# Loading a projection's weights in four later pieces and adding products of constants, in a recurrent-memory and linear-attention kernel

## The chip, the cores and the metric

The kernel runs as one program on one core of a Trainium2 chip. The metric is device time in microseconds of one execution. A core has five engines with their own instruction streams: TensorE (PE in the profile, with its weight loads listed as PEld), VectorE (DVE), ScalarE (ACT), GpSimd (POOL) and SyncE (SP). Here SP only issues DMA transfers; ACT and POOL issue some too. All DMA engines of the core are shared by all of these queues.

## The reference, cut to what matters

The input x is 2048 rows of 512. Four blocks follow each other, A, B, A, B, and each adds its result to x after a layer norm.

```
# A: 64 segments of 32 rows, 8 memory rows carried from one segment to the next
for s in range(64):
    h = concat([mem, xs])                       # 8 + 32 rows
    q, k, v = h @ Wq, h @ Wk, h @ Wv            # 32 heads of 128
    o = softmax(mask(q @ k.T * scale)) @ v
    o = o @ Wo                                  # back to 512
    mem = o[:8]; outs.append(o[8:])
# B: linear attention, 32 heads of 16
q, k, v = split(x @ wqkv);  pq, pk = phi(q), phi(k)   # phi: t+1 if t>0 else exp(t)
kv = pk.T @ v;  z = sum(pk)
out = ((pq @ kv) / (pq @ z)) @ wo
```

The memory rows make A a chain: a segment can't begin before the one ahead of it has passed through the output projection. B needs all rows of a block before its own output can be formed, since kv and z are sums over all 2048 rows.

## The kernel before, in words

The weights Wq, Wk, Wv and Wo (4 MB each) stay in SBUF for the whole run. SP issues their loads first: Wk, Wq and Wv as one transfer each, then Wo in 16 transfers of 256 KB, then wqkv (1.5 MB), the projection of block B, as one transfer (`load`, lines 1950 to 1962). ACT issues the memory rows and the first 128 rows of x, POOL the next two tiles of x.

A step is one segment of A. It projects the 40 rows to keys and queries (`project`, products at L2154, further ones with the weights that stay loaded at L2042), copies the results out of PSUM (L1919 on ACT, L1920 on DVE) and turns them by DVE transposes (L2173). Values are projected in the same way. `mem_attention` handles the part on which the next segment's memory depends (L2278, L2270, then L2304, L2306 and L2318). `out_block` is the output projection, 64 products with Wo (L2408); its two halves are added (L2419) and `next_mem` (L2436) turns the 8 new memory rows into columns for the next step. `x_attention` does the other rows beside the next step.

Every fourth row of x (the last 8 of each segment) is projected for four segments at once, the "left" blocks. In the opening, three of these are done before or beside step 0 (`first_left_blocks`: keys "sk", queries "sq", values "leftv").

Block B runs four steps behind A: `b_in` takes a tile of 128 rows through its layer norm, projects it with wqkv (`rows_of`, L2582) and adds to the sums kva and za. Its first use of wqkv is at 109.3 us. When all rows are there, `b_mid` forms four matrices zf (L2714) for the denominators and km (L2699), multiplies km with wo into MB (four products, copied out by L1920 or L1919), and `b_out` makes each tile: denominators (a product with zf), logarithm and exponential on ACT (L2811, L2813), the quotient on DVE (L2814), four products with MB and the sum on DVE (L2818). In the last block all 16 tiles come after the last segment; this is "the last memory tile's chain" with what follows it.

What sets the order: every operation is a node with a due time and, for copies, an engine, both from a table written into the kernel (`PLACE`). `schedule` sorts the nodes by due time, gives PSUM banks in that order, and each engine executes its nodes in that order, waiting on semaphores where a node needs another engine's result. A due time is no wait: an engine goes on as soon as its data are there. So the table decides order, the engine of a copy, and the PSUM bank, and nothing else.

The functions that the change touches follow.

Of the kernel before, what the change touches and what calls it, by code (L numbers as in the profile page):

```python
# [16 lines left out]
    (0, -9, 'setup'): '2751 2752 1621 15060 15061 16711 17238 20254 20902 21335 26596 31128 31613 36233 37053 37678 40093 41399 42472 43512 44808 60645 14865 0 560 1120 2190 2750 3310 17835 18402 18743 18744 18748 18959 18960 19391 20038 20470 21117 21333 21981 22197 22628 24910 25947 26595 27242 27673 27674 27675 27892 27891 29832 31127 32422 35143 39577a 17834 18745v 0 32839 35503 35506 36229 36234 29400 18746 0 0 0 0 0 0 0 0 0 0 0 0 0 0 0 0 0 0 0 0 0 0 0 0 0 0 0 0 0 0 0 0 0 0 0 0 0 0 0 0 0 0 0 0 0 0 0 0 0 0 0 0 0 0 0 0 0 0 0 0 0 0 0 0 0 0 0 0 0 0 0 0 0 0 0 0 0 0 0 0 0 0 0 0 0 27889 27890',  # L17
    (0, -4, 'start'): '19607a',
    (0, -2, 'leftv'): '37698 39210 39672 40371 41400a 41831 42471 42962a 44807 44810',
    (0, -2, 'prep'): '14142 14864 15059 15391 15647 16712 18006v 18749a 19393a 20471v 17833v',  # L20
    (0, -2, 'prepl'): '13340 14063 16713 18747 22198 22843 25550a',
    (0, 0, 'kq0'): '19821 20469 20901 22411 29615 29831 31126 31611 22843a 35502 32197v 34321',
    (0, 0, 'kq1'): '20685 22627 23714 26377 27672 28320 30046 30262 28751a 36228 34684v 32840a 35139',
    (0, 0, 'lq'): '730981 734917 735345 736139 737902 739038 739581 745577',
    (0, 0, 'lx'): '725135',
    (0, 0, 'mem0'): '36230 36232 37051 37314 37677 39560 40092 44809 43119 44811',
    (0, 0, 'mem1'): '36231 36726 37679 37681 42962 43400 43719 44806 45734 46451',
    (0, 0, 'next'): '48918 48972 49238v',
    (0, 0, 'out'): '45447 45515 46452 46605 46882 47101 47370 47588 48015a 48443',
    (0, 0, 'ql'): '35504a 34436a',  # L30
    (0, 0, 'sk'): '19390 21116 22196 23282 23707v 24430',
    (0, 0, 'sq'): '29183 29399 30910 31773 32197a 32838',
    (0, 0, 'v'): '39211 40967 41398 41830 42470a 44812a',
    (0, 0, 'x'): '38130 38346 38692 39560 39576 41401 40094 42262 48015 43282 43341 46451 48409 50344a 57004v 45446 46824 47807 48297 51423a 50345v',
    (0, 0, 'xl'): '1620',
    (0, 1, 'kq0'): '49480 49911 50343 50775 51855v 52419 51639a 52056',
    (0, 1, 'kq1'): '52419 52419 52501 52717 51206 51422 51638 51854 53141a 53782 52934a 52717a 52992',
    (0, 1, 'lq'): '756403 760618 760834 761049 762164 763460 764413 769975',
    (0, 1, 'mem0'): '52933 53423 53994 53795 54262 55249 55828 55830 55827 56230',
    (0, 1, 'mem1'): '53994 54876 55248 55829 55831 56230 56623 57442 56840 57443',  # L40
    (0, 1, 'next'): '59643 59697 59962a',
    (0, 1, 'out'): '56622 57003 57221 57440 58377 58378 58379 58717 58970a 59168',
    (0, 1, 'ql'): '40264a 39209v',
    (0, 1, 'res'): '65669 65917',
    (0, 1, 'sk'): '18958 20037 21332 21980 24908a 25549',
    (0, 1, 'sq'): '26161 26593 27456 28967 33316a 33958',
    (0, 1, 'v'): '52991 53523 54263 54444 55085v 56275a',
    (0, 1, 'x'): '55899 56274 57221 57444 57581 58716 58036 58376 59643 58718 58719 58969 59850 62803v 70329a 58851 58910 59168 59961 60644a 61939a',
    (0, 2, 'kq0'): '60212 60643 61075 61507 63018v 63151 62587a 63020',
    (0, 2, 'kq1'): '62802 63017 63290 63507 61938 62154 62370 62586 64587a 64588 63019a 63289a 63717',  # L50
    (0, 2, 'leftv'): '40535 42262 43511 44806 45446a 46088 47102 47371a 53348 57441',
    (0, 2, 'lq'): '762163 762379 763027 763243 764661 765609 767779 770110',
    (0, 2, 'lx'): '730981',
    (0, 2, 'mem0'): '63449 64586 65177 64958 65549 65916 66408 66717 66931 67239',
    (0, 2, 'mem1'): '64958 65176 65548 65668 65918 66158 66930 67238 67867 67868',
    (0, 2, 'next'): '70328 70382 70962v',
    (0, 2, 'out'): '67869 67870 67907 68125 68344 68562 68780 68999 69606a 69853',
    (0, 2, 'prep'): '15988 16710 16904 17237 17493 17968 18401v 26594v 20255a 24909v 29184a',
    (0, 2, 'ql'): '54469v 58910v',
    (0, 2, 'res'): '73922 79787',  # L60
    (0, 2, 'sk'): '19174 20253 21548 23498 27457a 27893',
    (0, 2, 'sq'): '28104 30478 30694 32421 35141a 35865',
    (0, 2, 'v'): '63723 64155 64959 65670 65916a 66933v',
    (0, 2, 'x'): '66408 66932 67451 67866 68781 69470 69130 68999 70496 69605 69853 69853 70753 75955a 81212v 69853 70436 70495 70641 70961a 71496v',
    (0, 3, 'kq0'): '71496 71537 72185 72616 73265a 73923 73921a 74831',
    (0, 3, 'kq1'): '73048 73696 74552 74559 70963 71969 73911 74127 75207a 75956 74551a 74830a 75955',
    (0, 3, 'lq'): '735345 757243 757954 760402 761049 762743 765002 785076',
    (0, 3, 'mem0'): '75206 75265 75836 75637 76342 77046 77047 77387 77180 77582',
    (0, 3, 'mem1'): '76343 76344 76658 77180 77045 77386 77975 78306 78192 78668',
    (0, 3, 'next'): '81044 81098 81364v',  # L70
    (0, 3, 'out'): '77974 78355 78573 78988 79060 79784 79785 79786 80399a 80569',
    (0, 3, 'ql'): '70193v 73911a',
    (0, 3, 'res'): '81365 89404',
    (0, 3, 'sk'): '18742 19606 21764 23066 27894a 28105',
    (0, 3, 'sq'): '31612 34437 35140 35142 37052v 37314',
    (0, 3, 'v'): '73264 74775 75837 75957 76659v 77388a',
    (0, 3, 'x'): '77386 77673 78027 78573 78987 79783 79442 79923 81098 80569 81211 81270 81364 85987a 86151a 80398 81152 81441 81499 86277v 86751v',
    (0, 4, 'kq0'): '81611 82043 82474 83122 83986v 84485 84485a 85065',
    (0, 4, 'kq1'): '82906 84486 84850 84851 83554 83769 83985 84485 85497a 85914 84904a 84849a 85332',
    (0, 4, 'lq'): '767175 767779 768593 774744 778783 779388 780112 785508',  # L80
    (0, 4, 'lx'): '754821',
    (0, 4, 'mem0'): '85496 85986 86358 87108 87110 87762 88094 88805 88311 88806',
    (0, 4, 'mem1'): '86518 86576 87327 87109 88311 88474 89023 89841 89022 90059',
    (0, 4, 'next'): '92261 92315 92581v',
    (0, 4, 'out'): '89403 89621 89840 90058 90276 90495 90713 90931 91358a 91786',
    (0, 4, 'ql'): '83987a 84848v',
    (0, 4, 'res'): '95415 97436 87107 87326 87544 87874 88092 88585 88804 89185 90495a 90713 92827 92824 95198 94120 92826 96826 94983 95199 97493',
    (0, 4, 'sk'): '25730 27241 27888 28536 30695v 30911',
    (0, 4, 'sq'): '32205 36835 37051 37680 38693v 38846',
    (0, 4, 'v'): '85064 85914 86151 86751 87763v 88093a',  # L90
    (0, 4, 'x'): '88585 91150 92825 92828 92829 94984 94119 94550 95414 96708 96825 97316 98357 99061a 100805v 96766 97375 97865 98804 102000a 104112a',
    (0, 4, 'xl'): '3810',
    (0, 5, 'kq0'): '92823 93254 93686 94118 95416a 96886 94982a 96885',
    (0, 5, 'kq1'): '94549 94765 94981 95197 95413 95628 95844 96060 96277a 97435 97434a 96484a 97866',
    (0, 5, 'lq'): '762595 763890 764412 765003 768386 771109 775937 776686',
    (0, 5, 'mem0'): '97433 97492 98359 97864 98708 100009 100144 100187 100143 100549',
    (0, 5, 'mem1'): '98277 98277 98911 98358 100008 101159 101478 101787 102002 102149',
    (0, 5, 'next'): '104710 104764 105030v',
    (0, 5, 'out'): '101014 101478 101489 102406 102543 102761 102979 103256 103683a 104111',
    (0, 5, 'ql'): '96827v 97437a',  # L100
    (0, 5, 'res'): '112945 107325',
    (0, 5, 'sk'): '25946 26809 27025 28751 30970a 31611',
    (0, 5, 'sq'): '32197 35505 37682 38130 39599a 40371',
# [1690 lines left out]
def _build_kernel(nc, A_x, A_mem0, A_Wq, A_Wk, A_Wv, A_Wo, A_seg_len, B_wqkv, B_wo, out):  # L1794
# [119 lines left out]
    add = P.add  # L1914
# [132 lines left out]
    def tiled(pe, o, w, x, start, stop, loaded=False):  # L2047

        for j in range(4):
# [3 lines left out]
            else:  # L2053
                r = pe.matmul(o[q], w[:, q], x, start=start, stop=stop, skip_group_check=True, tile_position=(0, 32 * j))  # L2054
        return r

    SPIN = {}
    LATE = {0: (8, 9, 10, 11, 12, 13, 6, 7, 4, 5), 1: (4, 5, 6, 7)}
    def spin(layer, step, name, units, cols=512, fresh=0):

# [818 lines left out]
```

## Time and profile before

| what | us |
|---|---|
| median of three runs (1575.15 to 1579.79) | 1576.27 |
| the profiled execution's own time | 1580.13 |
| its span, from first to last instruction | 1578.4 |
| PE busy (share of the span) | 1511.5 (96%) |
| DVE busy | 1223.1 (77%) |
| ACT busy | 987.4 (63%) |
| PE share of the chain that ended last | 83% |

The profile is of one execution. Times in its views are counted from the first instruction. "Idle before" names what ended the idle time of an engine; "issue" there means that the engine waited for nothing that the profile shows. PEclk is the share of the TensorE clock that was granted. The queue named q8 is that of instruction fetches.

### The profile page before, as it was taken

The page shows a single profiled execution, that of the slowest core. Times are in us where ns is not written, and L with a number is a line of the kernel's source. Part 1 is how long each engine was busy: PE and PEld are TensorE (multiplying, and loading weights), DVE is VectorE, ACT ScalarE, POOL GpSimd, SP SyncE. Part 2 cuts the span into 40 slices and gives each one's busy share as a digit, 9 for nine tenths or more (in the row PEclk, how much of TensorE's full clock was granted, in tenths as well). Part 3 has the DMA queues.
Part 4 walks back from the last instruction along what each step waited for, and adds up shares of the span by engine and source line. Part 5 has one row for each costly group of instructions (what it writes and reads, how often), then busy time and mean ns, then how long its engine had stood idle before and what let it go on. Part 6 is the DMA issues. An engine that isn't in the chain of part 4 may idle for free.

```text
span 1578.4 us, 97381 instructions
## 1 busy us (share of the span) xinstructions
PE 1511.5 (96%) x48481; PEld 822.8 (52%) x40705; DVE 1223.1 (77%) x3536; ACT 987.4 (63%) x3043; POOL 197.2 (12%) x396
## 2 busy tenths in 40 slices
PE   5899999999999999999999999999999999999997
PEld 2445555555555555555545555555555455555554
DVE  4577878887777788777878787888877787777778
ACT  2566665656666666665666666666576666576665
POOL 2011110111111011111111110111101011110110
PEclk9999999999999999999999999999999999999999
DMA  9301010110000000101310111111101111001124
GB/s 381 104 20 20 17 33 20 27 24 23 21 18 16 22 24 24 24 17 30 62 32 17 26 25 20 25 29 21 31 10 27 27 27 23 23 20 20 34 42 134
DMA packets 84819, 60.69 MB, mean 38 GB/s; under 512 B 64121, under 2 KB 78777, under 8 KB 82873
## 3 DMA queue, kind: packets, MB, share of 16 engines
q1 hardware_dynamic: 71096, 37.58, 9.7%
q0 software_dynamic: 13152, 16.75, 3.9%
q8 instruction: 349, 5.72, 1.5%
q14 instruction: 62, 0.50, 0.1%
q10 hardware_dynamic: 160, 0.14, 0.0%
HBM read 25.57 MB, written 11.67 MB: 24 GB/s over the span
## 4 chain that ended last, share of the span: by engine, by line
PE 83%; DVE 8%; ACT 4%; DMA 3%; issue 1%; POOL 0%; SPq 0%; DVEq 0%
PE pb L2154 31%; PE pb L2042 21%; PE pb L2408 18%; PE pb L2054 8%; PE pb L2582 2%; ACT arena_sb L1919 2%; DMA Wq_sb<-in_A_Wq_dram 2%; PE pb L2270 1%; DMA dx_sb<-y_sb 1%; DVE arena_sb L1920 1%; PE pb L2347 1%; PE pb L2436 1%; DVE arena_sb L2173 1%; DVE y_sb L2419 1%; DVE st_sb L2092 1%
## 5 line engine op out<-in xcount | busy, mean ns | idle before, releaser
L1919 ACT ACTIVATE arena_sb<-pb 128x512 bf16<-128x512 f32 (+5 forms) x1180 | 530.8, 483 | 320.4 <-PE pb L2042 162.1
L1920 DVE CAST arena_sb<-pb 128x512 bf16<-128x512 f32 (+4 forms) x591 | 297.7, 512 | 93.7 <-PE pb L2042 51.1
L2154 PE MATMUL pb<-Wk_sb,arena_sb 128*32 128x512 bf16 x4192 | 364.4, 383 | 5.5 <-ACT arena_sb L1919 3.3
L2408 PE MATMUL pb<-Wo_sb,arena_sb 128*32 128x256 bf16 x10368 | 337.6, 273 | 4.4 <-DVE arena_sb L2318 2.1
L2173 DVE STREAM_TRANSPOSE arena_sb<-arena_sb 128x256 f32<-128x256 f32 x640 | 266.2, 432 | 48.7 <-ACT arena_sb L1919 41.2
L2054 PE MATMUL pb<-arena_sb 128*32 128x128 bf16 (+2 forms) x10800 | 277.0, 208 | 14.8 <-DVE arena_sb L1920 4.9
L2408 PEld LDWEIGHTS pb<-Wo_sb,arena_sb 128*32 128x32 bf16 x10368 | 258.1, 96 | 48.7 <-DVE arena_sb L2318 14.7
L1936 POOL DMA_DIRECT2D dx_sb<-y_sb x246 | 125.3, 513 | 1152.4 <-DVE y_sb L2419 627.0
L2054 PEld LDWEIGHTS pb<-arena_sb 128*32 128x32 bf16 x10800 | 190.1, 95 | 147.5 <-issue 33.3
L2154 PE MATMUL pb<-Wq_sb,arena_sb 128*32 128x512 bf16 x3088 | 259.5, 382 | 1.5 <-DMA Wq_sb<-in_A_Wq_dram 0.4
L2042 PE MATMUL pb<-Wv_sb,arena_sb 128*32 128x512 bf16 x2560 | 251.6, 378 | 0.1
L2154 PE MATMUL pb<-Wv_sb,arena_sb 128*32 128x512 bf16 x2560 | 251.5, 378 | 0.1
L2154 PEld LDWEIGHTS pb<-Wk_sb,arena_sb 128*32 128x32 bf16 x4192 | 112.9, 97 | 193.2 <-issue 102.6
L2042 PE MATMUL pb<-Wq_sb,arena_sb 128*32 128x512 bf16 x2032 | 199.3, 380 | 0.0
L2154 PEld LDWEIGHTS pb<-Wq_sb,arena_sb 128*32 128x32 bf16 x3088 | 83.8, 97 | 97.2 <-issue 44.4
L1919 ACT ACTIVATE outW_sb<-pb 64x256 f32<-64x256 f32 x142 | 53.6, 378 | 106.0 <-PE pb L2408 90.1
L2419 DVE TENSOR_TENSOR y_sb<-pb,outW_sb 64x256 bf16<-64x256 f32 x162 | 68.7, 424 | 50.1 <-ACT outW_sb L1919 45.4
L2358 DVE TENSOR_TENSOR arena_sb<-arena_sb,bo_sb 128x512 bf16<-128x512 bf16 x256 | 103.5, 416 | 2.4
L2318 DVE TENSOR_TENSOR arena_sb<-pb,arena_sb 128x128 bf16<-128x128 f32 x252 | 72.9, 290 | 36.3 <-ACT arena_sb L2306 12.2
L2154 PEld LDWEIGHTS pb<-Wv_sb,arena_sb 128*32 128x32 bf16 x2560 | 70.5, 95 | 53.6 <-issue 29.5
L2042 PE MATMUL pb<-Wk_sb,arena_sb 128*32 128x512 bf16 x928 | 92.5, 379 | 0.0
L2293 DVE TENSOR_TENSOR arena_sb<-arena_sb 128x256 bf16<-128x256 bf16 x252 | 70.2, 281 | 24.2 <-ACT arena_sb L2285 21.1
(122 smaller groups left out, 1804.9 us busy)
## 6 DMA issues: line engine op xcount, KB each, us to landing
Wk_sb<-in_A_Wk_dram SPq DMA_DIRECT2D x1, 4096.0 KB, 13.7
Wq_sb<-in_A_Wq_dram SPq DMA_DIRECT2D x1, 4096.0 KB, 24.4
Wv_sb<-in_A_Wv_dram SPq DMA_DIRECT2D x1, 4096.0 KB, 34.1
Wo_sb<-in_A_Wo_dram SPq DMA_DIRECT2D x16, 256.0 KB, 7.4
xs_scratch<-x_sb POOLq DMA_DIRECT2D x32, 128.0 KB, 2.7
pq_scratch<-arena_sb POOLq DMA_DIRECT2D x27, 128.0 KB, 2.5
x_sb<-xs_scratch POOLq DMA_DIRECT2D x16, 128.0 KB, 3.3
dx_sb<-y_sb SPq DMA_DIRECT2D x126, 12.0 KB
```

The lines of the kernel that those rows point to most:

```text
L1919: return e.activation(o() if callable(o) else o, i() if callable(i) else i, ACTF.Copy)
L1920: return e.tensor_copy(o() if callable(o) else o, i() if callable(i) else i)
L1936: add(eng, lambda e: e.dma_start(o, i), 0.55 if eng == "pool" else 0.66, reads=reads, writes=writes, dsem="%s%d" % (kind, k), lat=lat + (0 ...
L2042: return pe.add_instruction(mybir.InstMatmult(name=nc.get_next_instruction_name(), engine=mybir.EngineType.PE, ins=[pe.lower_ap(x), pe.low ...
L2054: r = pe.matmul(o[q], w[:, q], x, start=start, stop=stop, skip_group_check=True, tile_position=(0, 32 * j))
L2154: r = pe.matmul(o, blk[:, c, :], w, start=(c == 0), stop=(c == 3), tile_position=(0, 32 * j))
L2173: add("dve", lambda v: v.transpose(dst, src(img[:, k, :].bitcast(F32))), 0.445, reads=[("img", k, h) for h in range(2)], writes=[dkey])
L2293: add("dve", lambda v: v.tensor_tensor(Pm[:, k, :].rearrange("p (a j x) -> p a j x", a=2, j=4), PQ[:, r2, b, 0:64].rearrange("p (a x) -> p ...
L2318: add("dve", lambda v: v.tensor_tensor(oTb[:, s % NO, 16 * b:16 * b + 16, 0:8].rearrange("p (i j) q -> p j i q", i=4), heads(pv.f32()[:, 0 ...
L2358: add("dve", lambda v, b=b: v.tensor_tensor(Pbx[:, :, b, :].rearrange("p j (k x) -> p j k x", k=4), px[:, b, :].rearrange("p (k x) -> p k ...
L2408: r = pe.matmul(tl.f32()[32 * j:32 * j + 32, 0:256], oT[:, 4 * hh + n, :], Wo_sb[:, 8 * n + hh, 256 * d:256 * d + 256], start=(hh == 0 and ...
L2419: add("dve", lambda e: e.tensor_tensor(y, tl.f32()[a, 0:256], outW[c, v, :], ALU.add), c_dve(256), reads=[("outW", w), "y0"], tiles=[tl], ...
```

## The change

Three things are edited, and the table of due times is written anew: every entry but one differs, so the order on every engine is another one throughout, though of the same kind.

First, wqkv is no longer loaded behind Wo. Each of the first four steps issues one of its four row blocks (384 KB) on SP, after that step's `next_mem` copy. All four write the one key "wqkv", so each also waits for the piece ahead of it.

Second, `spin` now makes n nodes of 12 products of the constant one_sb with itself (128x512, results never read). In the opening, 8 nodes stand before the left blocks' keys, once the first tile of x is there, with all 12 weights loaded anew; 4 stand between the left blocks' keys and the rest. The left blocks' first products are ordered behind the 8.

Third, in the last block 2 nodes stand behind the last tile's products and ahead of the four MB products, and 2 behind the first denominator product and ahead of tile 0's MB products.

In the new order ACT also issues the first tile of x ahead of the memory rows, and POOL issues its two tiles of x as its first instructions.

```diff
-    load(wqkv_sb[:, :, :], B_wqkv.rearrange("(c p) f -> p c f", p=128), "wqkv", 51.5)
+    P.count += 1
...
-    def spin(layer, step, name, units, cols=512, fresh=0):
+    def spin(layer, step, name, n, after=(), reads=(), fresh=1):
         P.at(layer, step, name)
...
+        for i in range(n):
+            tl = P.tile()
+            def mm(pe, tl=tl):
+                x = one_sb[:, 0:128].unsqueeze(1).to_broadcast([128, 4, 128])
+                for u in range(3):
+                    for j in range(4):
+                        o, q = tl.f32()[32 * j:32 * j + 32, 0:512], slice(32 * j, 32 * j + 32)
+                        if u < fresh:
+                            r = pe.matmul(o, one_sb[:, q], x, start=True, stop=True, skip_group_check=True, tile_position=(0, 32 * j))
+                        else:
+                            r = again(pe, o, one_sb[:, q], x, True, True, (0, 32 * j), True)
+                return r
+            nd = add("pe", mm, c_pe(3, 512), reads=["one"] + list(reads), tiles=[tl])
+            nd.order.update(after)
+            after = [nd]
+        return after
...
         def first_left_blocks():
+            done = []
+            last = spin(0, -3, "spin", 8, reads=[("x", 0)], fresh=3)
             for W, key, move, nm in ((Wk_sb, "Wk", left_keys, "sk"), (Wq_sb, "Wq", left_queries, "sq")):
                 for G in range(3):
                     for b in range(2):
                         at(2 * G + b, nm)
+                        n0 = len(P.nodes)
                         move(G, b, project(hTL[lroom(G)], [("hTl", lroom(G))], (W, key, b, True))[0])
+                        pe = [n for n in P.nodes[n0:] if n.engs == ("pe",)]
+                        if G == 0:
+                            for n in pe:
+                                n.order.update(last)
+                            done += pe
+                if nm == "sk":
+                    last = spin(0, -1, "spin", 4, done)
...
+            if first and s < 4:
+                nd = P.nodes[-1]
+                at(s, "ldqkv")
+                add("sp", lambda e, s=s: e.dma_start(wqkv_sb[:, s, :], B_wqkv.rearrange("(c p) f -> p c f", p=128)[:, s, :]), 0.45,
+                    after=[nd], writes=["wqkv"], dsem="dqkv%d" % s, lat=4.0)
...
     def b_mid(layer, step):
+        hold = []
+        if layer == 1:
+            hold = spin(layer, step, "spin", 2, [n for n in P.nodes[-40:] if n.engs == ("pe",) and n.key[2] == "bi"])
...
             add("pe", lambda pe, c=c, tl=tl: tiled(pe, tl.f32()[:, :], km[:, 128 * c:128 * c + 128], MB_sb[:, c, :], True, True),
-                c_pe(1, 512), reads=[kk, ("MB", c)], tiles=[tl])
+                c_pe(1, 512), reads=[kk, ("MB", c)], tiles=[tl]).order.update(hold)
...
-        add("pe", md, c_pe(4, 128), reads=["zf"] + ek + qk, tiles=[td])
+        nd = add("pe", md, c_pe(4, 128), reads=["zf"] + ek + qk, tiles=[td])
+        hold = []
+        if last and t == 0:
+            c, place = P.count, P.place
+            hold = spin(layer, step, "spin2", 2, [nd])
+            P.place, P.count = place, c
...
             add("pe", lambda pe, c=c: tiled(pe, ty.f32()[:, :], e[:, c, :], MB_sb[:, c, :], c == 0, c == 3),
-                c_pe(1, 512), reads=ek + [("MB", i) for i in range(4)], tiles=[ty])
+                c_pe(1, 512), reads=ek + [("MB", i) for i in range(4)], tiles=[ty]).order.update(hold)
```

## The prediction

> **What bounds the kernel now.** I read the page first: which engine is full, and what the chain that ended last consists of.
>
> ```profile
> PE 1511.5 (96%) x48481; PEld 822.8 (52%) x40705; DVE 1223.1 (77%) x3536; ACT 987.4 (63%) x3043; POOL 197.2 (12%) x396
> ...
> q8 instruction: 349, 5.72, 1.5%
> ...
> PE 83%; DVE 8%; ACT 4%; DMA 3%; issue 1%; POOL 0%; SPq 0%; DVEq 0%
> ```
>
> TensorE is busy 96% of the span and carries 83% of the chain, so a microsecond gained in the opening passes through the steps to the end, and an edit can only win where PE stands still or runs slowly. The middle line matters below: 48481 products and 40705 weight loads are 89186 PE instructions, and 349 packets fit 256 of them each. So q8 fetches PE's program in blocks of 256.
>
> Next, the table by windows around the two places that the change touches (columns: length, then busy time and instructions of PE, PEld, DVE, ACT, POOL, then the granted clock, the DMA share and GB/s).
>
> ```profile
> 26.20:29.60 3.40, 3.40 (x36) 1.33 (x32) 1.45 (x3) 1.23 (x3) 0.00 (x0) 0.50 1.01 422
> 50.00:53.50 3.50, 1.11 (x27) 0.49 (x23) 0.58 (x3) 0.98 (x2) 0.00 (x0) 1.00 0.08 26
> 53.50:56.90 3.40, 3.40 (x36) 1.03 (x24) 1.37 (x3) 0.60 (x1) 0.00 (x0) 0.50 0.00 0
> 64.50:1527.40 1462.90, 1427.85 (x46352) 778.06 (x38736) 1151.54 (x3363) 933.39 (x2918) 183.23 (x347) 1.00 0.11 24
> 1551.90:1555.40 3.50, 3.33 (x88) 2.10 (x80) 2.96 (x6) 2.30 (x4) 0.00 (x0) 0.51 0.23 75
> 1555.40:1578.40 23.00, 17.50 (x452) 8.96 (x444) 20.54 (x34) 16.02 (x29) 0.00 (x0) 1.00 0.28 93
> ```
>
> Three stretches of 3.4 us have half the clock. Each follows a 3.4 us stretch in which PE stood idle for 1.6 to 2.3 us. All else runs at 1.00, and between 64.5 and 1527.4 us PE is idle for only 35.05 us. Then the PE timeline, where step 0 hands over to step 1.
>
> ```profile
> 49.61 0.39 PE L2054 MATMUL pb<-arena_sb 128*32 128x128 bf16 x13
> 52.01 0.24 PE L2054 MATMUL pb<-arena_sb 128*32 128x128 bf16 x3 [2.01 <-issue]
> 52.02 0.26 PE L2436 MATMUL pb<-selm_sb,y_sb 128*32 128x16 bf16 x8
> ...
> 53.98 0.65 PE L2042 MATMUL pb<-Wq_sb,arena_sb 128*32 128x512 bf16 x4
> ```
>
> A group of 16 products breaks off after 13, and PE waits 2.01 us for nothing that the profile shows. The sum y that L2436 needs was ready at 50.2 (DVE L2419 at 49.77, 0.43 long). The packet records tell why: the fourth q8 fetch starts at 49.43 and ends at 50.59, and PE goes on 1.4 us later. Four other such stalls resume 1.3 to 1.6 us after a fetch ends (near 362, 635, 1208 and 1541 us), so the missing thing is code. PE had used up the block ahead at about 46.1, so this fetch started some 3.3 us late, while DMA carried 300 to 400 GB/s: the rest of Wo, and wqkv.
>
> ```profile
> arena_sb<-in_B_wqkv_dram SPq DMA_DIRECT2D x1, 1536.0 KB, 10.0
> ```
>
> That one transfer is the load that the change moves; its packets run from about 45.7 to 51 us, and the last piece of Wo lands at 47.7. At the end of the run it is DVE that has no air: 20.54 us busy of 23.00.
>
> ```profile
> 1541.99 0.39 PE L2054 MATMUL pb<-Wk_sb,arena_sb 128*32 128x512 bf16 x2 [1.09 <-issue]
> ...
> 1551.70 0.43 PE L2054 MATMUL pb<-Wq_sb,arena_sb 128*32 128x128 bf16 x16 [1.52 <-DVE arena_sb L2714]
> ```
>
> **The change part by part.** The sum is made against the profiled execution (span 1578.4, its own time 1580.13), and its difference is laid on the median of the runs, 1576.27, which lies 3.9 lower.
>
> (a) *The stall at 50.0.* In the new program L2436's counterpart is PE instruction 1483 instead of 1226, 257 more, so the block edge falls on the same spot, ten instructions ahead of it. The fetch is again asked for as the output projection begins, but only Wo's rest is ahead of it. It starts by 47.7 at the latest, and with 1.2 for the packet and 1.4 after it code is there by 50.3, at best by 49.5; it is needed at about 49.5. Bounds 0 to -2.01 (a fetch that comes as late as before, or none missed); I take -2.0, the fetch being asked for 46.5 to 47 and the stall then nil or a few tenths.
>
> (b) *The half clock from 53.5 to 56.9.* PE is on the chain throughout; 3.4 us at half clock do 1.7 us of work. Without the stall, PE idles some 0.4 us there and not 2.3. Bounds 0 to -1.7; I take -1.7.
>
> (c) *The products of constants in the opening.* 12 nodes of 12 products, four columns wide at 0.2155 us each (16 Wk products take 0.86): 36 x 0.2155 = 7.8 us of PE time. Cover: PE waits for Wq, which lands at 25.7. Before, PE begins at 13.24, idles 5.2 us until 36.87 (1.17 + 0.43 + 1.64 + 0.36 + 1.62) and loses 1.55 and 1.7 at half clock. After: ACT issues x ahead of the memory rows (0.80 instead of 1.43; the transfer issued at 0.80 began to move after 1.0 us, the one at 1.43 after 4.1), and POOL its tiles of x 1.0 to 1.6 us sooner. So the transposes stand at 9.5 to 11.5, and the products begin at 11.7 (bounds 11 and 13.5). From there: 24 groups of constants, 28 of Wk, 12 of constants, 13.8 us at full clock, 0.4 of transposes, and a slow start that costs 1.0 to 2.7, say 1.9: Wq's products begin at 27.8 and not 25.77. But they run at full clock: 32 groups, 6.9 us, end at 34.7, where before the like ended at 35.25. The attention of step 0, then 36.87, comes 0.6 sooner. Wo's landing at 47.7 allows at most 1.0: two last groups of the projection, L1919 0.38, L2419 0.43. If x lands as late as before and the slow start is long, +1.6. Bounds -1.0 and +1.6; taken -0.6. Without the wait for Wq, all 7.8 us would be on the path.
>
> (d) *The last chain.* From km (L2699, 1551.56) to the last sum, DVE works 23.8 of 24.6 us. The 2 + 2 nodes are 2.6 us of PE time. In the new order zf comes first, then three denominator groups (0.65), the constants (1.3), and the first MB product about 1.95 after zf; DVE has km, L2568 and two more to do until 2.6, so PE's extra is covered by DVE. If it weren't, up to 1.3 would lie on the path. What can go is DVE's 0.8 us of idle, of it 0.42 in the half-clock stretch. DVE's own work stays: 32 operations of about 0.6 are 19.2 us. Bounds -0.8 and +1.3; taken -0.7, nearer to the idle row. The stall of 1.09 at 1540.9 is a late fetch too, beside transposing DMAs that stay, and the block edge moves by some ten instructions only: I leave it.
>
> (e) *The four pieces.* Each is 384 KB, 0.9 us at 420 GB/s, issued once `next_mem`'s copy is done, with one in flight. In SP's queue stand behind them the DMAs that bring y's rows back to x, and the transposing DMA of the next layer norm; a piece waits for what is done by then, and the issue costs SP 0.67 where SP is idle. wqkv is used first at 109.3; pieces 1 to 3 stand between step 3's and step 4's row moves, at some 85 to 92. Cost 0, cover 17 us; if a fetch of code falls behind a piece, up to 0.9. On POOL nothing is moved but its two loads ahead of the memsets, 1.2 us later for constants that PE needs at 9.
>
> (f) *The new order of 126 steps.* The trace of before can't show it. It adds no work; it can spend or save PE's 35.05 us of idle. The largest gaps there are 1.01 at 784, 0.94 at 1184 and 1.36 at 1369: all three gone, -3.3; as many more, +3.3. Taken 0.
>
> Sum: -2.0 - 1.7 - 0.6 - 0.7 = -5.0, so 1571.3 us on the median.
>
> **Two rules weighed.** The row: five code stalls of 0.47 to 2.01 us in 349 fetches. The Trainium skill, "Runtime: NRT & Kernel Launch", section "Instruction fetch mechanics", has blocks of 256 instructions too, and says that crossing one is "mostly hidden". By that rule (a) and (b) are nil; the trace agrees for 344 fetches of 349, not for the one here. The row: half clock after 2.3 us of idle out of 3.4. "TensorE: Matmul & The Clock Gate", section "What's actually happening", also in the Trainium skill, asks for a whole idle window, and says that the windows run freely, so that the start of slow stretches differs from run to run. The trace denies the first; one trace can't show the second.
>
> **The rivals.**
> *The stall has another cause or stays.* The projection eats code at twice the usual rate (200 instructions from 47 to 50), and Wo is still moving when the fetch is asked for. Against it: no late fetch in the opening but the one behind wqkv. Then only (c) and (d): -1.3, 1575.0.
> *The slow stretches are luck.* If the runs that are timed have no half clock after the stall (two idle stretches on either side of a window's edge), (b) is gone: -3.3, 1573.0. For it: the runs are 3.9 us faster than the profiled execution.
> *The later fetch goes too.* The stall at 1540.9 and half of the middle's large gaps vanish: -5.0 - 1.1 - 1.6 = -7.7, 1568.6. For it only that order and edges have moved.
> *Slower: the new order of the middle costs.* Place: the memory chain of the 126 steps, where a copy now stands on the other engine or behind another. Price: one gap like those of 784 or 1184, about 1 us. It decides from ten more such gaps: -5.0 + 10 = +5, 1581.3. For it: every queue is reordered. Against it: 35 us of idle in 126 steps are 0.28 per step, and ten gaps would raise them by a third.
>
> **How the numbers follow.** The forecast has 0.45, with a range of its own of 1569 to 1573.5; rivals in order 0.14, 0.12, 0.15 and 0.14. What a measurement can tell from no change here is 0.3%, 4.7 us, so 1571.5 and 1581.0. Faster: two thirds of the forecast and the third rival, 0.30 + 0.15 = 0.45. Same: the rest of the forecast and the first two, 0.15 + 0.14 + 0.12 = 0.41. Slower: 0.14. The range leaves out most of the slower case and the lowest twentieth: 1567.0 (the third rival with the rest of (f)) to 1578.5 (forecast with (c), (d) and (f) at their upper ends).
>
> **What would show it.** Right: no gap before L2454 near 49, granted clock 1.00 from there to 64, the second `next_mem` near 60 instead of 64.5, four pieces landing before 95, DVE without idle from the first quotient on, PE idle of the middle near 35. Wrong: Wq's products later than 30, a fetch packet near 49 that starts more than 2 us after its block's edge, a slow stretch in steps 1 or 2, or a middle with over 40 us of idle.

## The result and the profile after

| | us |
|---|---|
| forecast | 1571.3 (1567.0 to 1578.5) |
| the changed kernel, median of six executions (1581.01 to 1586.97) | 1583.69 |
| the kernel before beside it, median of six (1575.15 to 1579.79) | 1576.91 |
| ratio, with its 95% interval | 1.0042 (1.0027 to 1.0057) |
| the profiled execution of the changed kernel, its own time | 1584.51 |

The change made the kernel slower, outside of the forecast's range and with the other sign. The size of the first timing was not repeated: in two later ones the ratio was 1.0017 both times (1.0005 to 1.0029, and 1.0007 to 1.0027). The kernel before had medians of 1580.2 to 1581.1 in four later groups; its first six executions were 3 to 4 us below that. So the loss is 2.7 us by the later timings and 6.6 by the first, where a gain of 5.0 was forecast.

The page of the changed kernel, the lines that answer those shown of before (busy time of the engines, the queue of code fetches, the chain that ended last):

```profile
PE 1519.9 (96%) x48673; PEld 837.6 (53%) x40833; DVE 1218.6 (77%) x3507; ACT 1002.0 (63%) x3072; POOL 197.7 (12%) x396
...
q8 instruction: 351, 5.75, 1.6%
...
PE 84%; DVE 7%; ACT 4%; DMA 3%; issue 2%; POOL 0%; SPq 0%; DVEq 0%; ACTq 0%; POOLq 0%
```

PE has 192 products more, the 16 nodes of 12, and 8.4 us more of busy time. ScalarE has 14.6 us more, VectorE 4.5 less: the new table put more copies on ScalarE. Next, windows of the changed kernel (length, busy time and instructions of PE, PEld, DVE, ACT and POOL, granted clock, DMA share, GB/s).

```profile
26.20:29.60 3.40, 3.40 (x72) 1.43 (x56) 0.98 (x3) 2.33 (x6) 0.00 (x0) 1.00 1.01 417
50.00:53.50 3.50, 3.14 (x80) 1.22 (x52) 1.69 (x6) 1.44 (x4) 0.00 (x0) 1.00 0.29 84
53.50:56.90 3.40, 3.40 (x105) 1.51 (x80) 2.52 (x8) 2.35 (x7) 0.00 (x0) 1.00 0.09 34
61.47:1532.74 1471.27, 1431.24 (x46361) 791.80 (x38745) 1147.20 (x3333) 949.49 (x2949) 183.49 (x347) 1.00 0.11 25
1551.90:1555.40 3.50, 2.97 (x117) 1.65 (x113) 3.08 (x10) 2.31 (x5) 1.10 (x2) 1.00 0.72 228
```

All three stretches at half clock are gone. But the middle, from the second `next_mem` to the last, takes 1471.27 us and not 1462.90, with practically the same number of products (46361 and 46352): the cost is there, not at the edited places. The PE timeline at the hand-over from step 0 to step 1 of the changed kernel:

```profile
50.31 0.40 PE L2050 MATMUL pb<-Wv_sb,arena_sb 128*32 128x512 bf16 x4
50.52 0.41 PE L2062 MATMUL pb<-arena_sb 128*32 128x128 bf16 x16
50.78 0.22 PE L2454 MATMUL pb<-selm_sb,y_sb 128*32 128x16 bf16 x8
```

The group of 16 products runs through, and `next_mem` (now L2454) follows at 50.78 without the stop of 2.01 us. By the starts of `next_mem`, the two profiles compare like this:

| stretch | before | after | difference |
|---|---|---|---|
| start to the first | 52.02 | 50.78 | -1.24 |
| first to second | 12.47 | 10.68 | -1.79 |
| second to last (the middle) | 1462.9 | 1471.3 | +8.4 |
| last to the end | 51.0 | 49.9 | -1.0 |
| span | 1578.4 | 1582.7 | +4.3 |

### The profile page after: what moved, and what is told of

Its sections match the earlier page's. It is cut to its first block, busy times and chain, and to the rows that moved or that the text cites. A ratio compares the mean times of both kernels' runs of the same rounds, so it can differ in the third digit from the quotient of the medians.

```text
span 1582.7 us, 97745 instructions
## 1 busy us (share of the span) xinstructions
PE 1519.9 (96%) x48673; PEld 837.6 (53%) x40833; DVE 1218.6 (77%) x3507; ACT 1002.0 (63%) x3072; POOL 197.7 (12%) x396
## 4 chain that ended last, share of the span: by engine, by line
PE 84%; DVE 7%; ACT 4%; DMA 3%; issue 2%; POOL 0%; SPq 0%; DVEq 0%; ACTq 0%; POOLq 0%
PE pb L2162 32%; PE pb L2050 21%; PE pb L2426 17%; PE pb L2062 8%; PE pb L2605 2%; PE pb L2288 2%; DMA dx_sb<-y_sb 1%; ACT arena_sb L1927 1%; DVE arena_sb L1928 1%; DMA arena_sb<-arena_sb 1%; PE pb L2365 1%; PE pb L2454 1%; DVE y_sb L2437 1%; DVE arena_sb L2181 1%; ACT outW_sb L1927 1%
## 5 line engine op out<-in xcount | busy, mean ns | idle before, releaser
L2162 PE MATMUL pb<-Wk_sb,arena_sb 128*32 128x512 bf16 x4192 | 368.2, 380 | 4.3 <-ACT arena_sb L1927 2.1
L1928 DVE CAST arena_sb<-pb 128x512 bf16<-128x512 f32 (+4 forms) x576 | 292.3, 515 | 81.4 <-PE pb L2050 46.3
L2162 PE MATMUL pb<-Wq_sb,arena_sb 128*32 128x512 bf16 x3088 | 264.5, 379 | 1.1 <-DVE arena_sb L1928 0.5
L2050 PE MATMUL pb<-Wq_sb,arena_sb 128*32 128x512 bf16 x2032 | 200.4, 379 | 0.0
L2162 PEld LDWEIGHTS pb<-Wq_sb,arena_sb 128*32 128x32 bf16 x3088 | 87.3, 96 | 94.9 <-issue 43.4
L2050 PE MATMUL pb<-Wk_sb,arena_sb 128*32 128x512 bf16 x928 | 93.8, 378 | 0.0
L2307 ACT ACTIVATE arena_sb<-pb 128x160 bf16<-128x160 f32 x256 | 77.3, 304 | 22.1 <-PE pb L2288 13.3
```

The source lines that it names most:

```text
L1928: return e.tensor_copy(o() if callable(o) else o, i() if callable(i) else i)
L2050: return pe.add_instruction(mybir.InstMatmult(name=nc.get_next_instruction_name(), engine=mybir.EngineType.PE, ins=[pe.lower_ap(x), pe.low ...
L2162: r = pe.matmul(o, blk[:, c, :], w, start=(c == 0), stop=(c == 3), tile_position=(0, 32 * j))
L2307: add("act", lambda a: a.activation(PQ[:, r2, b, 64:224], tl.f32()[:, 64:224], ACTF.Exp, scale=SCALE), c_act(160), tiles=[tl], writes=[("P ...
```

## The experiments

Four theories stood at the start. A: the edits gain, and the new order of the middle loses. B: the pieces, or code fetches that they delay, lose. B2: 257 more PE instructions shift the edges of the code blocks, and this loses. C: the slow stretches come and go by chance. "New" and "old" below are the tables of the changed kernel and of the kernel before; the middle is that between due times of 61 and 1516 us. Ratios are to runs of the kernel before on the same chip.

### One part at a time

The pieces alone, in the old order:

```diff
-    load(wqkv_sb[:, :, :], B_wqkv.rearrange("(c p) f -> p c f", p=128), "wqkv", 51.5)
+    P.count += 1
...
+            if first and s < 4:
+                nd = P.nodes[-1]
+                at(s, "ldqkv")
```

> Only the four pieces, in the order of before. Theory A (the edits gain, the new order of the middle loses): the stall of 2.0 us at the end of step 0 and the half clock behind it go, so 2 to 4 us less than before, and the stretch from the second to the last handover of memory rows is as long as before, 1463 us, within 1 us. Theory B (the pieces themselves, or the fetches of code that they delay, lose the time): the middle grows by 4 us or more and the run is 2 to 6 us slower than before. Theory C (the slow stretch at 53.5 us is luck that the timed runs mostly don't have): the profile gains as in A, the timed runs gain under 2 us.

Measured: 0.9983 (0.9973 to 0.9994), 2.7 us less, as A expects. The stop is gone, and the second `next_mem` follows the first after 10.68 us and not 12.47. The middle took 1464.95 us, 2.0 longer than before where A allowed 1; that is far from B's growth of 4, and the five profiles with the old middle span 1462.1 to 1465.0.

The opening's products alone, with x first, wqkv in one load and the old order:

```diff
+    (0, -3, 'spin'): '18005 18006 18007 18008 18009 18010 18011 18012',
+    (0, -1, 'spin'): '23301 24000 25000 26100',
...
+            last = spin(0, -3, "spin", 8, reads=[("x", 0)], fresh=3)
```

> Only the products of constants in the opening (8 and 4 nodes) and x issued first, in the order of before; wqkv as one load behind Wo. Theory A: the fetch that is late behind wqkv stays late, the products lie beside the wait for Wq; within 2 us of before. Theory B2 (the 257 further PE instructions shift the edges of the code blocks, and the stalls that follow lose the time): 3 us or more slower, in the middle.

Measured: 0.9993 (0.9980 to 1.0006), within the 2 us of theory A.

All edits, with the new opening and last chain, but the old middle (one entry of several thousand shown, against the changed kernel):

```diff
-    (0, 5, 'next'): '103766 103839 104085a',
+    (0, 5, 'next'): '104710 104764 105030v',
```

> The changed kernel's opening up to a due time of 61 us (its pieces and products included) and its last chain from 1516 us, with the order of before between them. Theory A: the middle is 1463 us again, opening 3 us and tail 1 us shorter than before, so about 4 us less than before in the profile, 2 to 4 in the timed runs, and 8 to 10 less than the changed kernel. Theory B or B2: the middle stays near 1471 us, and the run is 4 to 7 us slower than before.

Measured: 0.9983 (0.9970 to 0.9995). The middle is short again, but the last chain took 52.65 us from the last `next_mem` to the end, 1.7 longer than before and not 1 shorter; why is told further down, with the seams.

None of the edits, old opening and last chain, but the new middle (against the kernel before):

```diff
-    (0, 5, 'next'): '104710 104764 105030v',
+    (0, 5, 'next'): '103766 103839 104085a',
```

> The opening (wqkv behind Wo, no products of constants) and the last chain of before, with the changed kernel's order from a due time of 61 us to 1516 us. Theory A: the middle alone carries the loss, 1471 us instead of 1463, so 7 to 10 us slower than before. Theory B or B2: within 2 us of before.

Measured: 1.0040 (1.0025 to 1.0056), 6.3 us, a little under the 7 to 10 expected, with a middle of 1467.5 us and not 1471. The middle of the kernel with all edits and old order, and that of the kernel with new order and no edit, by windows:

```profile
61.70:1523.83 1462.13, 1427.24 (x46360) 779.37 (x38744) 1150.92 (x3365) 933.61 (x2917) 183.27 (x347) 1.00 0.12 25
```

```profile
61.78:1529.31 1467.53, 1428.34 (x46352) 785.88 (x38736) 1146.47 (x3330) 949.14 (x2951) 183.36 (x347) 1.00 0.11 24
```

A holds, B and B2 fall. The pieces and the 257 instructions are in the first of these and it is not slow; neither is in the second, and it alone loses as much as the whole change did in its first timing.

### Order, or the engines of the copies?

The new table moves nodes in time and gives 726 copies of the middle to the other engine. The changed kernel with the old engines in the middle, and its counterpart, all edits in the old order with the new engines (the second diff is against the kernel with all edits and the old middle):

```diff
-    (0, 5, 'next'): '103766 103839 104085a',
+    (0, 5, 'next'): '103766 103839 104085v',
```

> The changed kernel, with its order of nodes, but in the middle (due times of 61 to 1516 us) every copy out of PSUM goes back to the engine that it had before: 726 of some 2300 copies change between ScalarE and VectorE. Theory A1, the order of the nodes loses: a ratio to the kernel before near 1.004, as the whole change. Theory A2, the engines of the copies lose (ScalarE has 15 us more of work in the middle, and the sum y waits 53.0 us for ScalarE's copies and not 45.4): 0.998, as the four edits in the old middle. Theory A3, order and engines were fitted to each other, and any mixture of two tables loses: 1.005 or more, so above the whole change.

```diff
-    (0, 5, 'next'): '104710 104764 105030v',
+    (0, 5, 'next'): '104710 104764 105030a',
```

> The reverse: the four edits of the change in the order of the middle of before (0.9983 with the old engines), with the engine of 728 copies as in the change. TensorE's instructions stand in the same order as in that kernel. A1, the order: 0.998. A2, the engines: 1.004. A3, the fit between both: 1.005 or more.

Measured: 1.0276 (1.0247 to 1.0304) and 1.0392 (1.0367 to 1.0417). Theory A3 holds, and by far more than it asked for. Neither half of the table is the bad one: a table's order and its engines belong together. The waits of PE show how a mixture fails. From the view of waits, the memory attention's products waiting for VectorE's turns (total us, times, longest), over the whole run of the mixture with new order, of that with new engines, and of the changed kernel:

```profile
PE pb L2296 <- DVE arena_sb L2181: 9.9, 18, 1.7
```

```profile
PE pb L2296 <- DVE arena_sb L2181: 13.8, 32, 1.7
```

```profile
PE pb L2296 <- DVE arena_sb L2181: 5.7, 7, 1.7
```

In the middle PE is idle for 65.2 and 73.4 us in the mixtures, and for 40.0 in the changed kernel. That is not all of the loss: PE's busy time there is 17.5 and 23.5 us longer, for the same products. In the mixture with new engines TensorE executes the same order as the fast kernel with all edits and the old middle, and the mean record of a product is 279 ns in both. So by the records its products aren't slower; they overlap less, and part of the waiting stands in the profile as busy time.

PSUM banks are given out in the nodes' order, so "order" includes them; no run takes the banks apart from it.

### Where in the middle?

The new middle in the first layer only, and in the second only, with all edits in both (diffs against the changed kernel):

```diff
-    (1, 20, 'next'): '1024278 1024332 1024751v',
+    (1, 20, 'next'): '1023821 1023875 1024140a',
```

> The changed kernel with its order and engines up to the end of the first layer's segments (due times to 750 us), and those of before from there to 1516 us. Steps of the two kernels with the new middle last 3.4 us longer in the first layer and 2.1 in the second than in the four kernels with the old one. Loss spread over the run: 0.998 + 3.4 / 1578 = 1.000, middle of the first layer longer by some 3.4 us and the second as before. Loss in one spot of the first layer (steps 9 to 23 hold 2.5 us): the first layer again, 1.000 to 1.002. Loss by something global (code edges, phase): 1.002 to 1.004 whichever layer is reordered.

```diff
-    (0, 5, 'next'): '103766 103839 104085a',
+    (0, 5, 'next'): '104710 104764 105030v',
```

> The reverse: order and engines of before from 61 to 750 us, those of the change in the second layer. Loss spread over the run: 0.998 + 2.1 / 1578 = 0.9995, and the steps (1,20) to (1,22) each 0.6 to 0.8 us longer. Loss only in the first layer: 0.998. Loss by something global: 1.002 to 1.004.

Measured: 1.0011 (0.9996 to 1.0026) and 0.9993 (0.9979 to 1.0008). Against the 0.9983 of all edits with the old middle, the first layer costs some 4.4 us. The second costs 1.6, which the intervals can't tell from nothing; that the loss is in both layers rests on the profiles, where the steps with the new table take 3.4 us more in the first layer and 1.6 in the second. For the steps listed here the length goes with the table that the step is run by, in every profile. Lengths in us, lowest and highest, worked out from the starts of `next_mem`; a step runs from its own `next_mem` to the next:

| step | old middle, 5 profiles | new middle, 6 profiles | new in layer 0 only | new in layer 1 only |
|---|---|---|---|---|
| (0,4) | 12.36 to 12.74 | 11.59 to 11.77 | 11.75 | 12.36 |
| (0,5) | 11.02 to 11.41 | 11.75 to 12.38 | 11.75 | 11.26 |
| (0,33) | 10.76 to 10.77 | 11.34 to 11.75 | 11.37 | 10.76 |
| (1,20) | 11.24 to 11.25 | 11.69 to 12.06 | 11.25 | 11.69 |
| (1,30) | 11.49 to 11.50 | 10.95 to 10.99 | 11.54 | 10.95 |

Step (1,20) shows the mechanism. From the timelines of before (start, length, engine, and in brackets the idle time ahead): ScalarE's copy of `next_mem`'s result, VectorE's sum beside it, and PE's first product with the new memory rows.

```profile
1035.62 0.20 ACT L1919 ACTIVATE arena_sb<-pb 128x32 bf16<-128x32 f32 x1 [0.42 <-PE pb L2054]
...
1035.75 0.69 DVE L2818 TENSOR_TENSOR x_sb<-x_sb,pb 128x512 bf16<-128x512 bf16 x1
...
1035.87 0.40 PE L2154 MATMUL pb<-Wk_sb,arena_sb 128*32 128x512 bf16 x4 [0.26 <-ACT arena_sb L1919]
```

In the changed kernel the same copy is VectorE's, and the same sum of 0.69 us (now L2849) stands ahead of it, in the table as `'1024278 1024332 1024751v'` for `'1023821 1023875 1024140a'`:

```profile
1039.11 0.69 DVE L2849 TENSOR_TENSOR x_sb<-x_sb,pb 128x512 bf16<-128x512 bf16 x1
1039.72 0.18 DVE L1928 CAST arena_sb<-pb 128x32 bf16<-128x32 f32 x1
...
1039.96 0.40 PE L2162 MATMUL pb<-Wk_sb,arena_sb 128*32 128x512 bf16 x4 [0.53 <-DVE arena_sb L1928]
```

PE waits 0.53 us for the copy and not 0.26. Later in the step it waits 0.64 and 0.31 us for VectorE, where the kernel before waits 0.16 and 0.28 us for VectorE and ScalarE. Together that is 0.78 us more, and the step is 0.80 us longer (12.05 and 11.25). With the new table in the second layer alone the step is only 0.44 us longer, under the 0.6 to 0.8 expected. Of the 124 steps of the middle 45 are over 0.1 us longer in the mean of the new profiles and 27 over 0.1 shorter; all increases are 15.9 us, all decreases 10.9, and the difference is the loss: 5.0 us.

### The change again, and its parts taken out of it

The unchanged changed kernel, then without the last chain's products, and with one load of wqkv:

> The changed kernel itself, beside the next three. In the profile of the change its middle (second to last next_mem) lasted 1471.3 us; with the same order in the middle the old opening had 1467.5. If 3.7 of this is chance (row moves that land late, code fetches that come late), the middle now lasts 1466 to 1469 and the ratio to before stays at 1.003 to 1.0045. If it belongs to the program, it is 1471 again. Either way the steps (0,4) and (1,20) to (1,22) differ from before's by the same -0.9 and +0.4 to +0.8 us, since the order sets them.

Measured: 1.0017 (1.0005 to 1.0029), and a middle of 1467.3 us. So about 4 of the 8.4 us by which the two first profiles differ belong to that one execution, not to the program. In step (0,12), for one, the first profile waits 1.64 us because VectorE had stood 2.70 us for a transfer of y's rows; this profile has no such wait.

```diff
-            hold = spin(layer, step, "spin", 2, [n for n in P.nodes[-40:] if n.engs == ("pe",) and n.key[2] == "bi"])
+            hold = []
...
-            hold = spin(layer, step, "spin2", 2, [nd])
+            hold = []
```

> The change without the 2 + 2 products of constants in the last memory tile's chain. Step (d) of the prediction: they are worth 0.7 us, by a slow stretch of 3.4 us at half clock near the first quotients that comes back and lets VectorE wait again; time +0.7 against the change, from the last next_mem to the end 50.6 and not 49.9. Rival, the slow stretch of before was luck: no slow stretch, +0 to -0.3.

Measured: 1.0020 (1.0006 to 1.0033), beside 1.0017 with these products. From the last `next_mem` to the end it is 49.9 us with and without them. Its windows there have the clock at 1.00 throughout:

```profile
1551.40:1554.80 3.40, 2.87 (x120) 1.65 (x112) 2.95 (x11) 2.07 (x4) 1.10 (x2) 1.00 0.62 201
1554.80:1581.40 26.60, 19.59 (x533) 10.68 (x528) 24.34 (x43) 19.08 (x34) 0.00 (x0) 1.00 0.30 99
```

The products in the last chain do nothing that can be seen.

```diff
-    P.count += 1
+    load(wqkv_sb[:, :, :], B_wqkv.rearrange("(c p) f -> p c f", p=128), "wqkv", 51.5)
```

> The change with wqkv loaded again as one transfer behind Wo. Steps (a) and (b) of the prediction: the code fetch near 49 stands behind that transfer, TensorE stops for 2.0 us and then runs 3.4 us at half clock: the second next_mem 3.7 us later (65.2 and not 61.5), ratio to the change 1.0023. Rival, the half clock is luck of the window's edge: only the stop, 0.9 to 2.0 us, no slow stretch (as in the two runs with one load so far, which stopped for 0.98 us): +1.0 to +2.0, ratio to the change 1.0006 to 1.0013.

Measured: 1.0013 (1.0002 to 1.0024); the intervals can't tell it from the change, at 1.0017. So what the pieces gain in the old order (0.17%) these runs don't show in the new one. Its PE timeline has the code stop again, in the same group of 16 products, but of 1.19 us, and the window after it is at full clock:

```profile
51.93 0.24 PE L2062 MATMUL pb<-arena_sb 128*32 128x128 bf16 x4 [1.19 <-issue]
51.99 0.22 PE L2454 MATMUL pb<-selm_sb,y_sb 128*32 128x16 bf16 x8
```

```profile
53.80:57.20 3.40, 3.40 (x88) 1.39 (x64) 1.85 (x5) 2.34 (x7) 0.00 (x0) 1.00 0.00 0
```

The rival holds as to size: the stop belongs to the load, and half clock need not follow. With one load the stop was 2.01, 0.98, 0.98 and 1.19 us in four profiles, and only the first, the longest, had half clock behind it; in the twelve profiles with pieces there is neither at this place. The second `next_mem` comes 1.1 us later than in the run of the change beside it (62.69 against 61.60), not 3.7.

### A version from the better stretches, and one without the new order

All edits, with the new table up to step (0,9) and from (1,26) to (1,34), and the old one elsewhere in the middle (the diff is against the changed kernel):

```diff
-    (0, 33, 'next'): '422683 422737 423003v',
+    (0, 33, 'next'): '423168 423530 423533a',
```

> The four edits of the change, with the stretches of the new order that were shorter in three profiles of three: the new order and engines up to step (0,9) (-1.2 us by then) and from (1,26) to (1,34) (-1.1), those of before elsewhere. If what a step takes goes with the order and engines of that step alone: 0.9983 less 2.3 / 1578, so 0.997, faster than both kernels. If each seam costs as a mixture of tables does: 1.000 or more.

Measured: 0.9999 (0.9985 to 1.0013). Seams cost: step (1,33), at a seam, took 15.06 us where both tables have 12.97 or 13.67. So does the seam at 1516 us: from the last `next_mem` to the end, kernels with a middle and a last chain from different tables took 51.3 to 52.7 us (four profiles), those with both from one table 49.7 to 51.4 (ten). So the two hybrids of the first comparison, all edits in the old middle and the new middle without edits, each carry in their profiles some 2 us that belong to their seam. The timings don't show it for the first: the kernel without that seam, next, is at 0.9981 and not 0.9983.

The pieces and the opening's products, with old middle and old last chain (diff again against the changed kernel), and the change once more beside it:

```diff
-            hold = spin(layer, step, "spin2", 2, [nd])
+            hold = []
...
-    (1, 62, 'next'): '1514326 1514380 1515028v',
+    (1, 62, 'next'): '1513717 1513771 1514037v',
```

> The four pieces and the opening's products of constants with the middle and the last chain of before. Pieces alone were 0.9983, the opening's products alone 0.9993. If the gains add up (the stop near 50 gone: 1.0 to 2.0 us; the slow stretch at 26 gone: 0.6 to 1.0): 0.9975, and the kernel with both and the new last chain lost its share in that chain (52.7 us from the last next_mem to the end, with 3.4 of code stops, where before had 51.0). If the opening's products gain nothing beside the pieces: 0.9983.

> The changed kernel a third time. By the parts measured so far: the edits with the old middle -2.7 us, the new order in the first layer +4.4 over them, in the second +1.6, together +3.3 and a ratio of 1.002. If the first timing stands, 1.004.

Measured: 0.9981 (0.9970 to 0.9993) and 1.0017 (1.0007 to 1.0027). The first has no seam in the last chain and yet gains no more than the pieces alone: the opening's products add nothing that these runs can tell from zero. It beats both kernels, by 0.19% and 0.36%. It is 3.1 us faster than before; add 5.0 for the new middle, and 1.9 us is what the change should lose, or some 1 us if the new last chain is counted, which is 0.9 us shorter in the profiles. It lost 2.7 in the two later timings, which agrees within their intervals, and 6.6 in the first, which these parts don't account for.

## Why the prediction was wrong, step by step

*(f), the new order of 126 steps*, "adds no work", "Taken 0", failed. In the two profiles that were compared the middle is 8.4 us longer. Over all profiles it is 1463.6 us in the mean with the old table (five, 1462.1 to 1465.0) and 1468.7 with the new one (six, 1467.3 to 1471.3): +5.0, beyond the bound of 3.3. Of this 1.3 are waits of PE for other engines (33.8 to 35.1), 1.7 stops of over 0.15 us in which it waits for nothing that the profile shows (2.3 to 3.9, between 1.7 and 5.6 from one profile to the next), and 2.1 busy time (1427.6 to 1429.7). The last part isn't slower products, as far as the records tell (the profile models the ends of products): their mean is 279.2 ns in all eleven profiles and the clock is at 1.00, so the same products overlap less. What holds them apart, no run shows. The sign of being wrong that the prediction named, a middle with over 40 us of idle, came in the first profile, if barely (40.03); the mean of the six is 39.0. The bound was the wrong kind. It was set by the largest single gaps, but 72 of 124 steps moved by over 0.1 us in one direction or the other, and the sum of so many small changes is not limited by the three largest. That idle time of 0.28 us per step leaves little to gain was a reason to expect a loss: where little can be won, most other orders are worse. This is an argument and not a measurement; the mixtures only show how far down it can go, 44 to 62 us.

*The rival "the new order of the middle costs"* is what happened, with its place (a copy on the other engine or behind another) as in step (1,20). Its form was wrong: not ten gaps of 1 us, but many small ones, as the 0.27 us by which that copy comes later. Its chance of 0.14 was the error of judgement. What spoke for it could be read off the two tables: every queue reordered, and 726 of some 2300 copies on the other engine, which the prediction didn't count.

*(a), the stop at 50.0*, was right in mechanism and, for the two profiles compared, in size. Code is asked for when the projection begins, and finds the queues free: the fetch starts at 47.21 (47.7 at the latest was forecast) and not at 49.43. But 2.01 was the largest of four stops at this place; 1.0 to 1.2 is usual. The rival that the stop has another cause fell: the stop is in four of four profiles with the single load and in none of twelve with the pieces.

*(b), the half clock at 53.5*, was right for the two profiles, and luck: of the four profiles with the stop only that of before has half clock behind it. From the first to the second `next_mem` it took 12.47 us, in the other fifteen profiles 10.68 to 10.78. So 1.7 us is more than the change saves in the mean, and the rival "luck" comes nearer.

*(c), the opening's products*, has the wrong sign in these profiles. Without its stop the first `next_mem` of before would be at 50.0, and with the pieces alone it is at 50.06; after, it is at 50.8, and in the eleven profiles that have the new opening and the pieces at 50.3 to 51.6. x came as forecast (products from 11.98, 11.7 expected), but the first 96 took 7.78 us and not 5.2: a group of four took 0.43 us until 16.9 us and 0.22 after that, so the slow start cost 2.6, where 1.9 was taken. Wq's products begin at 28.7 and not at 27.8, and the attention of step 0 is 0.75 us later (37.62 against 36.87) and not 0.6 sooner. The products do keep the clock: the slow stretch near 26 is in all three profiles with the old opening and in none of thirteen with the new. A slow stretch near 38 to 42 is new in six of these thirteen, behind a wait of 1.7 us for VectorE's turns.

*(d), the last chain*, had about the right size (-1.0 for -0.7) by the wrong cause: the chain is as short without its products. What goes with the shorter chain is its new order: a half-clock stretch between 1545 and 1556 us is in four of the five profiles with the old last chain and in none of the eleven with the new one.

*(e), the four pieces*, was right: they are issued at 51.3, 72.9, 76.2 and 83.7 us and have landed at 54.3, 76.1, 79.3 and 87.7, the rows of wqkv are not missed, and the pieces alone gain 0.17% in the old order.

The range missed because it was built around the edits, whose costs were known to a microsecond, while the table, of which the trace of before shows nothing, got a bound of the same size. By the prediction's own terms the upper end should have been 1578.8 and not 1578.5, which changes nothing.

## What to carry to other kernels

Where a change comes with a new order of a long, nearly full stretch, the order is the larger part of the forecast: set its cost by how many steps move, not by the largest gap, and expect a loss where little idle time is left to win. Keep an edit and a new order apart when measuring; here the best kernels have the old middle, with the pieces alone (0.9983), with the opening's products as well (0.9981) or with all edits (0.9983), and these runs can't tell the three apart. In this kernel an order and its assignment of work to engines are fitted to each other, and taking over one without the other cost 2.8 and 3.9%.

## What the runs showed of the hardware

The same idle time is followed by half clock in some executions and not in others. The changed kernel itself, profiled three times, had half clock at 39.4 to 42.8 us once and not the other two times, though the idle time ahead was the same 1.73 + 0.85 us in all. The Trainium skill, "TensorE: Matmul & The Clock Gate", section "What's actually happening", says that the window runs freely and that the point of transition varies with its phase; these profiles agree, which one trace could not show. Taken together, the 16 profiles show more. In each of them the clock changes lie on one grid of 3.413 us. Within the runs all ten windows of that grid with more than 2.0 us of PE idle time are followed by half clock, none of the 7316 with less than 1.6 us is, and of the 16 between these four are. So what counts is how much of the idle time falls into one window. That fits the stops near 50 us: the 2.01 us of before left 2.31 us idle in its window, the stop of 1.19 us with one load 1.57 (the ends of products are modelled, so the border is rough):

```profile
50.71:54.12 3.41, 1.84 (x48) 0.61 (x31) 0.96 (x4) 0.49 (x1) 0.00 (x0) 1.00 0.03 8
54.12:57.53 3.41, 3.41 (x88) 1.48 (x68) 2.18 (x6) 2.54 (x7) 0.00 (x0) 1.00 0.00 0
```

The mean granted clock is a usable meter for this. Over 108 executions of the kernel before it is 0.9977, over 22 of the changed kernel 0.9994, and over 10 with the old opening and the new middle 0.9976: so it isn't the new middle that holds the clock up. The opening's products alone bring it to 0.9989, the pieces alone to 0.9980, and both with the old last chain to 0.9987; the rest comes with the new last chain (0.9992 with the old middle between). Among those 108, a clock higher by 0.001 went with 0.8 us less; the two only go together, and no run changes the clock alone. By that the clock is worth 1.4 us, less than the new order cost.

A stop for code of 1.1 to 2.2 us, as the last segment ends (1540.9 us before, 1545.7 after), is in all 16 profiles, whichever table is used; each time PE goes on 1.3 to 1.6 us after the packet of a code fetch has ended. No run tried to remove it.
